# Gated linear attention, a mixer and two MLPs on one core: the first batch in whole 128-token chunks, weight conversion in single steps

## Chip, core and metric

The kernel runs on one core of one Trainium2 chip. The metric is device time in microseconds, the median of several runs; the matrix engine is TensorE (PE in the profile, its weight loads PEld), the others are VectorE (DVE), ScalarE (ACT), GpSimd (POOL) and SyncE (SP), whose queue issues the DMAs.

## What is computed

Attention over 4 batches of 8 heads, 768 tokens, 48 values a head, with a state that decays by a sigmoid gate; then a low-rank mixing over the tokens (rank 32) and an MLP 384 to 1536 to 384, both with a residual; then a gated MLP with width 1024. Cut to what matters:

```python
f = 1.0 / (1.0 + np.exp(-f_logit))
for t in range(S):
    state = f[:, :, t, :, None] * state + einsum('bhd,bhe->bhde', k[:, :, t], v[:, :, t])
    y[:, :, t] = einsum('bhd,bhde->bhe', q[:, :, t], state)
u = x + (x^T @ U @ V)^T                      # x: y of all heads side by side
x = u + max(u @ w_ch1, 0) @ w_ch2            # first MLP
h = max(x @ w_in, 0)                         # second MLP
out = (h * sigmoid(conv3(h) * conv_w)) @ w_out
```

The weights arrive as 64-bit floats, the rest as 32-bit floats.

## The kernel before

**Attention** works in 24 chunks of 128 tokens, six to a batch. For a chunk g, `gates` makes ln(1 + exp(-f)) on ScalarE, `prefix` sums it over the tokens with a triangular matmul into `n`. VectorE evicts `b` (a clamp), ScalarE takes exp from the same bank (`a`), then exp of `b`; GpSimd multiplies q by `a` (`qh`) and k by `b` (`kh`). `transpose` turns both (`qTp`, `kTp`) and ScalarE copies them out. The sums restart at the middle of a chunk: each chunk is two halves of 64 tokens with a state update each, and `scores`, `state` and `values` work in 64 x 64 quarters of the array, two heads and two halves apart. A head's v is needed on both partition halves, so a second copy `vs` with the halves exchanged is loaded. The last row of `a` of each half goes to DRAM (`ends`) and comes back over the partitions (`ends_back`, `ga`) as the state's decay. `mix_in` multiplies the chunk's y by U into `z` and transposes it into `u32`; after six chunks `mix_z` and six `mix_out` add the mixing. All of it is a generator, `chunk(i)`, that yields after each step: seven to a chunk.

**Weights.** A 128-column piece of a 64-bit weight (393 KB) is made into a 32-bit float by three integer instructions on VectorE (L117 to L119), split into two parts by a copy on ScalarE and a subtraction on GpSimd. `Queue.tick(n)` writes n of these steps and the split of the piece before; two pieces are loaded ahead into three buffers. Conversion and attention share the instruction streams in the order in which this is written; nothing reorders it.

**Lead.** In the first stretch attention alone is written, chunks 0 to 5 and the mixing of batch 0, one conversion step after each yield: 54 steps. `fill` adds a matmul that computes nothing needed ahead of transposes and mixing, from the eleventh step on.

**First MLP.** Units of `up1` (tile `a`, then `rh` on ScalarE, `rl` on VectorE) and `down1` (tiles `b`), in 12 pieces j of 128 columns, two tokens' tiles a batch: 512 and 256 tokens for batch 0, 384 twice after that. Nine matmuls a half unit. A half unit ends in a yield, where the main loop writes conversion steps (three as long as there are any), checks of the weights' range, and attention steps of the next batch by a running budget `due`. Before batch 3's units the rest of attention is written and the weights of the second MLP begin to be converted.

**PSUM** has eight banks; `rot` deals out those that transposes, prefix sums and mixing share, two of them (7 and 3) in the lead.

Of the kernel before, what the change touches and what calls it, by code (L numbers as in the profile page):

```python
# [20 lines left out]
LEAD = 1  # L21
# [11 lines left out]
def kernel(  # L33
# [23 lines left out]
    NG = B * NCH  # L57
    N_WHOLE = LEAD * NCH + 2
    NP = H // 2
# [407 lines left out]

    rots = [[7, 3]]

# [41 lines left out]
    ft, qt, kt, vt, vs = {}, {}, {}, {}, {}  # L511
    sph, spl, bt = {}, {}, {}

    def load(dst, src, nm, g):
        if g >= NG:
            return
        b, c = divmod(g, NCH)
        t = {"v": ld_v, "f": ld_f}.get(nm, ld_p).tile([128, H, D], F32, tag=nm, name=nm)
        nc.sync.dma_start(out=t, in_=src[b, :, c * C:(c + 1) * C, :].rearrange("h t d -> t h d"))
        dst[g] = t  # L520
        if nm == "v":


            t = ld_v.tile([128, NP, D], F32, tag="vs", name="vs")
            sv = src[b].rearrange("(a j) t d -> j t a d", j=2)
            for j in range(2):
                at = c * C + (1 - j) * HC
                nc.sync.dma_start(out=t[j * HC:(j + 1) * HC], in_=sv[j, at:at + HC])
            vs[g] = t
# [8 lines left out]
    def gates(g):  # L538
        if g >= NG:
            return  # L540
        sp = spt.pop(g)
        nc.scalar.activation(out=sp, in_=sp, func=ACTF.Exp, scale=-1.0)
        nc.scalar.activation(out=sp, in_=sp, func=ACTF.Ln, bias=one, scale=1.0)

        if g < N_WHOLE:
            sph[g] = sp
            return
        h_ = wk1.tile([128, H, D], F32R, tag="sph", name="sph")
        l_ = wk1.tile([128, H, D], F32R, tag="spl", name="spl")
        nc.scalar.copy(out=h_, in_=sp)  # L550
        sph[g], spl[g] = h_, l_
        sub(nc.vector if g < 4 else nc.gpsimd, l_, sp, h_.bitcast(F32))

    def fill(ps, n=1):


        m, cols = ps.shape[0], min(math.prod(ps.shape[1:]), NCH * 2 * R)
        flat = ps.rearrange("p a b -> p (a b)") if len(ps.shape) == 3 else ps
        for _ in range(n if filling[0] else 0):
            mm(flat[:, 0:cols], tri_r[:, 0:m], uhl.rearrange("p c r -> p (c r)")[:, 0:cols], True, True)  # L560

    filling = [False]

    def prefix(g):
        n = bank(rot(), [128, DM], "n")
        if g >= N_WHOLE:
            mm(n, tri_r, sph.pop(g).rearrange("p h d -> p (h d)"), True, False)
            mm(n, tri_r, spl.pop(g).rearrange("p h d -> p (h d)"), False, True)
        else:
            mm(n, tri, sph.pop(g).rearrange("p h d -> p (h d)"), True, True)  # L570
        nv = n.rearrange("p (h d) -> p h d", h=H)
        b_ = wk1.tile([128, H, D], F32, tag="b", name="b")
        nc.vector.tensor_scalar(out=b_, in0=nv, scalar1=EXP_LIMIT, scalar2=None, op0=ALU.min)
        nc.scalar.activation(out=heads(a_t[g % 2]), in_=nv, func=ACTF.Exp, scale=-1.0)  # L574
        eng = nc.vector if g < 2 else nc.gpsimd
        eng.tensor_tensor(out=heads(q_t[g % 2]), in0=qt.pop(g), in1=heads(a_t[g % 2]), op=ALU.mult)  # L576

        def rest():
            nc.scalar.activation(out=b_, in_=b_, func=ACTF.Exp)
            eng.tensor_tensor(out=heads(k_t[g % 3]), in0=kt.pop(g), in1=b_, op=ALU.mult)  # L580

        return rest
# [9 lines left out]
    def ends(g):  # L592
        for x in range(2):
            r = (x + 1) * HC - 1
            nc.sync.dma_start(out=ends_d[g, x], in_=a_t[g % 2][r:r + 1].rearrange("o p d -> o (p d)"))

    def ends_back(g):
        with nc.allow_non_contiguous_dma(reason="rows over the partitions"):
            nc.sync.dma_start(out=ga[0:MP, g, :], in_=ends_d[g].rearrange("x o (p d) -> d (x o p)", d=128)[0:MP])

    qT, kT, sc, pt, wt, yt = {}, {}, {}, {}, {}, {}

    def transpose(g, nm):
        src, dst = (q_t[g % 2], qT) if nm == "qT" else (k_t[g % 3], kT)
        ps = bank(rot(), [MP, NP, C], nm + "p")
        fill(ps)
        for p in range(NP):
# [13 lines left out]
    def scores(g):  # L621

        kk, qq = kT.pop(g), qT[g]
        ps = bank(2 if g <= LEAD * NCH else 4, [128, NP, 2, HC], "s")
        for p in range(NP):
# [9 lines left out]
    def state(g):  # L635
        kh, vv = k_t[g % 3], vt[g]
        last = (g + 1) % NCH == 0
        ps = [bank((0 if g < LEAD * NCH else 4) + x, [MP, NP, D], f"kv{x}") for x in range(1 if last else 2)]
        for x in range(len(ps)):
# [22 lines left out]
    def values(g):  # L662
# [15 lines left out]
        for j in range(2):  # L678
            nc.scalar.copy(out=av[:, :, j, :], in_=ps[j].rearrange("t (p d) -> t p d", d=D))
        if g < LEAD * NCH:  # L680
            return
        h_ = wk1.tile([128, DM], F32R, tag="xh", name="xh")
# [3 lines left out]
        xh[g], xl[g] = h_, l_  # L686

    zps = {}

    def mix_in(g):  # L690
        b, c = divmod(g, NCH)
        if c == 0:
# [8 lines left out]
        ps = bank(rot(), [128, KD, C], "xT")  # L701
        fill(ps)
        for m in range(KD):
# [27 lines left out]
    def mix_out(b, i):  # L731
        m, hf = divmod(i, 2)
        ps = bank(rot(), [128, HF], "mix")
        fill(ps, 1 if i else 4)
        mm(ps, zst[b][:, m * 128:(m + 1) * 128], vst[:, hf * HF:(hf + 1) * HF], True, True)
# [59 lines left out]
    def chunk(i):  # L795
# [5 lines left out]
        if new:  # L801
            values(i - 1)
            yield
# [37 lines left out]
        if new:  # L841
            for x in range(2 * KD):
                mix_out(i // NCH - 1, x)
                yield
                if x > 1 and x % 2 == 0 and (i == NCH or LEAD == 1):
                    parts["split_tile"](i // NCH - 1, 0, [x // 2 - 1])
            if i == NCH or LEAD == 1:
                parts["split_tile"](i // NCH - 1, 0, [KD - 1])
# [4 lines left out]
    def attention():  # L853
        for i in range(NG + 1):
            yield from chunk(i)

    with tc.manual_schedule():
# [4 lines left out]
            compare_op=ALU.is_ge, fill=0.0,  # L862
        )
        nc.gpsimd.memset(tri[0:HC, HC:C], 0.0)
        nc.vector.memset(one, 1.0)
# [6 lines left out]
        nc.vector.memset(k_t[0], 0.0)  # L872
        nc.vector.tensor_copy(out=tri_r, in_=tri)
        for t, x in ((q_t[1], 0.0), (k_t[1], 0.0), (a_t[1], 1.0), (k_t[2], 0.0)):
            nc.gpsimd.memset(t, x)
# [29 lines left out]
        gates(2)  # L905

        att = attention()
        for n in range(10 ** 6):
            next(att)
            weights.tick(1)  # L910
            filling[0] = n > 10
            if len(mixed) == LEAD:
                break
        filling[0] = False
        rots[0] = [7, 0]
# [6 lines left out]
        late_q = None  # L922
        running = True
        for what, b in half_units:
            if what == "tile":
# [4 lines left out]
                else:  # L930
                    while running and len(mixed) < b + LEAD:
                        if next(att, "end") == "end":
                            running = False
                    left_att, left_hu = n_att if b + LEAD < B else 0, 4 * J1
                assert b in mixed
                if b == B - LEAD:
                    while running and next(att, "end") != "end":
                        pass
                    weights.flush()
                    assert not weights.left()  # L940
                    for _ in checks:
                        pass

                    nc.vector.tensor_reduce(out=g1[:, 0:1], in_=ga.rearrange("p g a -> p (g a)"), axis=mybir.AxisListType.X, op=ALU.min)
                    nc.vector.tensor_reduce(out=g1[:, 1:2], in_=bad, axis=mybir.AxisListType.X, op=ALU.max)
                    nc.vector.scalar_tensor_tensor(
                        out=g1[:, 0:1], in0=g1[:, 1:2], scalar=0.0, in1=g1[:, 0:1], op0=ALU.is_equal, op1=ALU.mult)
                    gs.close()
                    ws_p = ws.enter_context(tc.tile_pool(name="ws_p", bufs=2))
                    weights = Queue(ws_p, parts["open_late"]())  # L950
                    weights.fetch(2)
                continue
            left_hu -= 1
            if LEAD > 1 and left_hu == 10 and b < B - 1:
                parts["split_tile"](b + 1, 0)
            if b >= B - LEAD:
                if left_hu < 4 * J1 - 6 or b > B - LEAD:
                    weights.tick(2 if LEAD == 1 else 1)
                if b == B - LEAD and left_hu == 4 * J1 - 8:
                    ps = bank(rot(), [1, 128], "gp")  # L960
# [11 lines left out]
            if not busy:  # L972
                next(checks, None)
            due += (0.6 if busy else left_att / max(left_hu - 4, 1))
            while due >= 1 and left_att > 0 and running:
# [181 lines left out]
```

## Time and profile before

| | us |
|---|---|
| median of three runs | 719.91 |
| lowest, highest | 719.77, 720.64 |
| the profiled execution | 719.37 |
| its span in the profile | 717.4 |
| first matmul of the first MLP | 93.48 |
| first matmuls of the second MLP | 502 |

| engine | busy us | share |
|---|---|---|
| TensorE | 681.3 | 95% |
| VectorE | 450.4 | 63% |
| ScalarE | 298.1 | 42% |
| GpSimd | 148.4 | 21% |

Matmuls overlap, so a busy TensorE is not yet one at its peak. The chain that ended last is TensorE for 81% of the span, VectorE for 9%, ScalarE for 4%.

### The profile page before, as it was taken

What the parts mean: (1) busy time and instruction counts of PE and PEld (TensorE: products, weight loads), DVE (VectorE), ACT (ScalarE), POOL (GpSimd) and SP (SyncE); (2) the same over time, 40 slices, a digit from 0 to 9 for tenths busy, and PEclk for the clock granted to TensorE, in tenths of its full rate; (3) what the DMA queues carried; (4) which work ended last, traced back from release to release, by engine and by line L of the source; (5) the groups of instructions that cost most, each with busy time, mean ns of one, the idle gap of its engine ahead of it and who ended that gap; (6) DMA issues with size and microseconds to landing.
All of it is one profiled execution on the core that took longest, in us unless ns stands there. A gap on an engine that the chain in (4) does not pass through costs nothing.

```text
span 717.4 us, 15034 instructions
## 1 busy us (share of the span) xinstructions
PE 681.3 (95%) x6260; PEld 627.0 (87%) x6260; DVE 450.4 (63%) x749; ACT 298.1 (42%) x608; POOL 148.4 (21%) x147
## 2 busy tenths in 40 slices
PE   6988789999999999999999999999899999999996
PEld 4656577878899989999998999999899999999996
DVE  5679889334654534444433437888787877877763
ACT  4556443335444434424523213224444544535542
POOL 1246553214222222112300002223001001001000
PEclk9769789999999999999999999999999999999999
DMA  7799754435455254234210102331000100100102
GB/s 153 159 210 209 184 144 99 95 74 113 95 117 128 65 108 93 62 78 102 50 35 2 45 0 67 97 102 45 0 1 1 67 1 0 67 1 1 67 0 71
DMA packets 158000, 53.96 MB, mean 75 GB/s; under 512 B 138012, under 2 KB 153396, under 8 KB 157924
## 3 DMA queue, kind: packets, MB, share of 16 engines
q1 hardware_dynamic: 157924, 52.92, 31.4%
q8 instruction: 51, 0.84, 0.5%
q14 instruction: 25, 0.20, 0.1%
HBM read 48.08 MB, written 4.82 MB: 74 GB/s over the span
## 4 chain that ended last, share of the span: by engine, by line
PE 81%; DVE 9%; ACT 4%; issue 3%; DMA 2%; SPq 1%; POOL 0%; DVEq 0%; ACTq 0%; POOLq 0%
PE a L71 35%; PE b L71 32%; PE y L71 3%; PE s L71 3%; PE kv L71 2%; DVE u L118 1%; DVE ul L74 1%; PE n L71 1%; DMA u<-in_moe_w_ch_dram 1%; PE z L71 1%; PE kTp L608 1%; PE qTp L608 1%; PE xT L704 1%; DVE u L117 1%; DVE u L737 1%
## 5 line engine op out<-in xcount | busy, mean ns | idle before, releaser
L255 DVE SCALAR_TENSOR_TENSOR rl<-a,rh 128x384 fp32r<-128x384 f32 (+2 forms) x96 | 53.4, 556 | 147.9 <-ACT rh L254 147.8
L254 ACT ACTIVATE rh<-a 128x384 fp32r<-128x384 f32 (+2 forms) x96 | 47.1, 490 | 167.7 <-PE a L71 167.5
L71 PE MATMUL a<-uh,w1h 128*128 128x384 f32 (+2 forms) x288 | 103.0, 358 | 3.1 <-DVE rl L255 1.4
L71 PE MATMUL b<-rh,w2h 128*128 128x384 f32 (+2 forms) x288 | 101.1, 351 | 0.0
L71 PE MATMUL a<-ul,w1h 128*128 128x384 f32 (+2 forms) x288 | 97.9, 340 | 0.0
L71 PE MATMUL a<-uh,w1l 128*128 128x384 f32 (+2 forms) x288 | 97.7, 339 | 0.0
L71 PE MATMUL b<-rh,w2l 128*128 128x384 f32 (+2 forms) x288 | 97.0, 337 | 0.0
L71 PE MATMUL b<-rl,w2h 128*128 128x384 f32 (+2 forms) x288 | 96.6, 336 | 0.0
L71 PE MATMUL b<-woh,w1h 128*128 128x384 f32 x264 | 70.4, 334 | 0.0
L71 PE MATMUL a<-uh,winh 128*128 128x384 f32 x192 | 65.7, 342 | 1.8 <-ACT h L307 1.8
L71 PE MATMUL a<-ul,winh 128*128 128x384 f32 x192 | 66.1, 344 | 1.1 <-DVE ul L74 1.1
L71 PE MATMUL a<-uh,winl 128*128 128x384 f32 x192 | 65.8, 343 | 0.0
L71 PEld LDWEIGHTS a<-uh,w1h 128*128 128x128 f32 x288 | 54.4, 189 | 8.0 <-DVE u L737 2.6
L74 POOL TENSOR_TENSOR ul<-u,uh 128x384 fp32r<-128x384 f32 (+2 forms) x16 | 19.6, 1232 | 201.7 <-ACT uh L95 201.7
L71 PEld LDWEIGHTS b<-rh,w2h 128*128 128x128 f32 x288 | 54.2, 188 | 2.6 <-issue 0.3
L71 PEld LDWEIGHTS a<-uh,w1l 128*128 128x128 f32 x288 | 54.4, 189 | 1.7
L71 PEld LDWEIGHTS a<-ul,w1h 128*128 128x128 f32 x288 | 54.5, 189 | 1.2
L71 PEld LDWEIGHTS b<-rh,w2l 128*128 128x128 f32 x288 | 54.1, 188 | 1.5
L71 PEld LDWEIGHTS b<-rl,w2h 128*128 128x128 f32 x288 | 54.3, 189 | 1.1
L313 ACT ACTIVATE c<-c 128x768 f32<-128x768 f32 x31 | 26.3, 847 | 64.8 <-DVE c L343 64.8
L576 POOL TENSOR_TENSOR qh<-q,a 128x384 f32<-128x384 f32 x22 | 23.9, 1086 | 137.5 <-ACT a L574 117.2
L71 PEld LDWEIGHTS b<-woh,w1h 128*128 128x128 f32 x264 | 48.0, 188 | 0.0
(154 smaller groups left out, 1409.1 us busy)
## 6 DMA issues: line engine op xcount, KB each, us to landing
u<-in_moe_w_ch_dram SPq DMA_DIRECT2D x24, 384.0 KB
raw<-in_moe_w_ch_dram SPq DMA_DIRECT2D x24, 384.0 KB
f<-in_f_logit_dram SPq DMA_DIRECT2D x24, 192.0 KB
k<-in_k_dram SPq DMA_DIRECT2D x24, 192.0 KB
q<-in_q_dram SPq DMA_DIRECT2D x24, 192.0 KB
v<-in_v_dram SPq DMA_DIRECT2D x24, 192.0 KB
out_dram<-o SPq DMA_DIRECT2D x24, 192.0 KB
raw<-in_moe_w_in_dram SPq DMA_DIRECT2D x8, 384.0 KB
```

The source lines that it names most:

```text
L71: nc.tensor.matmul(out=out, lhsT=lhsT, rhs=rhs, start=start, stop=stop, skip_group_check=True)
L74: eng.tensor_tensor(out=out, in0=a, in1=b, op=ALU.subtract)
L117: lambda: ve.tensor_scalar(out=t, in0=hi, scalar1=3, scalar2=0x3FFFFFFF, op0=ALU.logical_shift_left, op1=ALU.bitwise_and),
L118: lambda: ve.scalar_tensor_tensor(out=t, in0=hi, scalar=-(1 << 30), in1=t, op0=ALU.bitwise_and, op1=ALU.bitwise_or),
L254: nc.scalar.activation(out=rh, in_=ps, func=ACTF.Relu)
L255: nc.vector.scalar_tensor_tensor(out=rl, in0=ps, scalar=0.0, in1=rh.bitcast(F32), op0=ALU.max, op1=ALU.subtract,)
L313: nc.scalar.activation(out=c, in_=c, func=ACTF.Sigmoid)
L576: eng.tensor_tensor(out=heads(q_t[g % 2]), in0=qt.pop(g), in1=heads(a_t[g % 2]), op=ALU.mult)
L608: nc.tensor.transpose(out=ps[:, p, :], in_=src[:, p, 0:MP], identity=ident)
L704: nc.tensor.transpose(out=ps[:, m, :], in_=x[:, m * 128:(m + 1) * 128], identity=ident)
L737: nc.vector.tensor_tensor(out=dst, in0=ps, in1=dst, op=ALU.add)
```

## The change

Batch 0 (`N_WIDE`, six chunks) is taken out of the generator and written by a new function `wide(i)`. There a chunk is whole: the prefix sums run over all 128 tokens, `scores_wide` makes 128 x 128 scores for two heads at a time on halves of the array, each head row with its bank and mask (`mask_wide`), `state_wide` updates the state once, `values_state` and `values_chunk` make y in two parts. `vs` and the first `ends` are not loaded and stored for these chunks. `prefix` is written ahead of the two masks, and a chunk holds three conversion steps instead of about seven. The first MLP starts after the same point of chunk 7 as before. In the main loop attention steps count 0.25 for each half unit instead of 0.6 as long as weights are left, range checks go twice as fast, and the second MLP's weights begin from within batch 3's units. The fillers are gone. Gates 6 and 7 are split in two like the later ones. The core of the diff (the new functions whole but for `state_wide`'s and `values_out`'s ends):

```diff
-    N_WHOLE = LEAD * NCH + 2
+    N_WIDE = LEAD * NCH
-    rots = [[7, 3]]
+    rots = [[0, 1]]
-        if nm == "v":
+        if nm == "v" and g >= N_WIDE:
-    def fill(ps, n=1):
...
     def ends(g):
         for x in range(2):
+            if x == 0 and g < N_WIDE:
+                continue
...
-        ps = bank(2 if g <= LEAD * NCH else 4, [128, NP, 2, HC], "s")
+        ps = bank(4, [128, NP, 2, HC], "s")
...
+    def scores_wide(g):
+        kk, qq = kT.pop(g), qT[g]
+        ps = sw[g] = [bank(2 + j, [128, NP, C], f"s{j}") for j in range(2)]
+        for p in range(NP):
+            for j in range(2):
+                mm(ps[j][:, p, :], kk[rows(j), p, :], qq[rows(j), p, :], True, True)
+        pt[g] = []
+
+    def mask_wide(g, j):
+        t = wk2.tile([128, NP, C], F32, tag="p", name="p")
+        nc.vector.tensor_tensor(
+            out=t, in0=sw[g][j], in1=tri.unsqueeze(1).to_broadcast([128, NP, C]), op=ALU.mult)
+        pt[g].append(t)
+
+    def state_wide(g):
...
+        ps = src = bank(7, [MP, NP, D], "kv")
+        for p in range(NP):
+            for j in range(2):
+                m = 64 if j == 0 else D
+                mm(ps[64 * j:64 * j + m, p, :], kh[:, p, 64 * j:64 * j + m], vv[:, 2 * p + j, :], True, True)
...
+    def values_state(g):
+        ps = yw[g] = [bank(4 + j, [128, NP * D], f"y{j}") for j in range(2)]
+        qq = qT.pop(g)
+        if g % NCH:
+            w = wt.pop(g)
+            for p in range(NP):
+                for j in range(2):
+                    mm(ps[j][:, p * D:(p + 1) * D], qq[rows(j), p, :], w[rows(j), p, :], p == 0, False)
+
+    def values_chunk(g):
+        ps, vv, pp = yw[g], vt.pop(g), pt.pop(g)
+        for j in range(2):
+            for p in range(NP):
+                mm(ps[j][:, p * D:(p + 1) * D], pp[j][:, p, :], vv[:, 2 * p + j, :],
+                   p == 0 and g % NCH == 0, p == NP - 1)
...
+    def wide(i):
+        load(kt, k, "k", i + 3)
+        load(qt, q, "q", i + 3)
+        load(ft, f_logit, "f", i + 4)
+        load(vt, v, "v", i + 2)
+        if i > 0:
+            values_out(i - 1)
+        scores_wide(i)
+        if i + 2 < NG:
+            second = prefix(i + 2)
+        mask_wide(i, 0)
+        mask_wide(i, 1)
+        state_wide(i)
+        gate_max(i + 3)
+        if i + 2 < NG:
+            ends(i + 2)
+        weights.tick(1)
+        if i + 1 < NG:
+            transpose(i + 1, "qT")
+            transpose(i + 1, "kT")
+        if i + 2 < NG:
+            second()
+        gates(i + 3)
+        values_state(i)
+        weights.tick(1)
+        if i > 0:
+            mix_in(i - 1)
...
+        values_chunk(i)
+        weights.tick(1)
+        if i + 2 < NG:
+            ends_back(i + 2)
...
-        for i in range(NG + 1):
+        for i in range(N_WIDE, NG + 1):
             yield from chunk(i)
...
+        for i in range(N_WIDE):
+            wide(i)
+        rots[0] = [7, 0, 1]
         att = attention()
-        for n in range(10 ** 6):
+        while len(mixed) < 1:
             next(att)
             weights.tick(1)
-            filling[0] = n > 10
...
-                    left_att, left_hu = n_att if b + LEAD < B else 0, 4 * J1
+                    left_att, left_hu = n_att + (10 if b + LEAD == B - 1 else 0) if b + LEAD < B else 0, 4 * J1
...
-                if left_hu < 4 * J1 - 6 or b > B - LEAD:
-                    weights.tick(2 if LEAD == 1 else 1)
+                since += 1
+                if since > 2:
+                    weights.tick(2)
...
             if not busy:
                 next(checks, None)
+                next(checks, None)
-            due += (0.6 if busy else left_att / max(left_hu - 4, 1))
+            due += (0.25 if busy else left_att / max(left_hu - 4, 1))
```

How the instructions stand. First VectorE in the lead, in one chunk: `p` is the masked scores, `b` the eviction of the prefix sums, `sp` the gates' clamp, `u32` the buffer in which L117 to L119 convert. Before:

```order
L630 TENSOR_TENSOR p_645<-s_628,msk_98 128x512
L118 SCALAR_TENSOR_TENSOR u32_63<-u32_63 128x384
L573 TENSOR_SCALAR b_650<-n_648 128x384
L536 TENSOR_SCALAR sp_656<-f_479 128x384
L119 SCALAR_TENSOR_TENSOR u32_63<-u32_63 128x384
L117 TENSOR_SCALAR u32_63<-u32_63 128x384
```

After (two lines further up in the file, so that L116 to L118 convert):

```order
L562 TENSOR_SCALAR b_637<-n_634 128x384
L691 TENSOR_TENSOR p_641<-s0_624,tri_96 128x512
L691 TENSOR_TENSOR p_643<-s1_625,tri_96 128x512
L706 TENSOR_TENSOR wtmp_654<-kv_645,w_550 112x192
L708 TENSOR_TENSOR w_656<-wtmp_654,ga_99 112x192
L535 TENSOR_SCALAR sp_658<-f_512 128x384
L116 TENSOR_SCALAR u32_63<-u32_63 128x384
L117 SCALAR_TENSOR_TENSOR u32_63<-u32_63 128x384
L118 SCALAR_TENSOR_TENSOR u32_63<-u32_63 128x384
```

The eviction `b` has moved ahead of the masks, conversion steps have moved from between them to the chunk's end.

Second, SP's queue in the lead, from one `ends_back` on. Before, to the next one:

```order
L599 DMA ga_99<-ends_d_106 112x8x1
L519 DMA k_475<-in_k_dram 128x8x48
L519 DMA q_477<-in_q_dram 128x8x48
L519 DMA f_479<-in_f_logit_dram 128x8x48
L106 DMA u32_63<-in_moe_w_ch2_dram 128x768
L595 DMA ends_d_106<-a0_111 1x512 x2
L519 DMA v_555<-in_v_dram 128x8x48
L528 DMA vs_557<-in_v_dram 64x4x48 x2
L106 DMA u32_63<-in_moe_w_ch1_dram 128x3x256
L599 DMA ga_99<-ends_d_106 112x8x1
```

After, up to the one weight load of the chunk:

```order
L591 DMA ga_99<-ends_d_106 112x4x1
L518 DMA k_410<-in_k_dram 128x8x48
L518 DMA q_412<-in_q_dram 128x8x48
L518 DMA f_414<-in_f_logit_dram 128x8x48
L518 DMA v_416<-in_v_dram 128x8x48
L586 DMA ends_d_106<-a0_111 1x512
L105 DMA u32_63<-in_moe_w_ch2_dram 128x768
```

`vs` and one of the two `ends` are gone, `v` has moved to the other loads, and one weight load is left of two or three.

Third, VectorE in the first MLP tile, between the `rl` of the eighth and of the ninth up unit. Before (`raw` and `bad` are a range check, `wtmp` and `w` the state):

```order
L255 SCALAR_TENSOR_TENSOR rl_1704<-a_1705,rh_1703 128x512
L165 TENSOR_TENSOR raw_1665<-raw_1665 128x384
L652 TENSOR_TENSOR wtmp_1736<-kv0_1718,w1_1464 112x192
L654 TENSOR_TENSOR w0_1738<-wtmp_1736,ga_99 112x192
L652 TENSOR_TENSOR wtmp_1740<-kv1_1719,w0_1738 112x192
L654 TENSOR_TENSOR w1_1742<-wtmp_1740,ga_99 112x192
L167 SCALAR_TENSOR_TENSOR bad_105<-raw_1665,bad_105 128x384
L630 TENSOR_TENSOR p_1785<-s_1768,msk_98 128x512
L255 SCALAR_TENSOR_TENSOR rl_1788<-a_1789,rh_1787 128x512
```

After:

```order
L254 SCALAR_TENSOR_TENSOR rl_1327<-a_1328,rh_1326 128x512
L118 SCALAR_TENSOR_TENSOR u32_63<-u32_63 128x384
L116 TENSOR_SCALAR u32_63<-u32_63 128x384
L117 SCALAR_TENSOR_TENSOR u32_63<-u32_63 128x384
L118 SCALAR_TENSOR_TENSOR u32_63<-u32_63 128x384
L116 TENSOR_SCALAR u32_63<-u32_63 128x384
L117 SCALAR_TENSOR_TENSOR u32_63<-u32_63 128x384
L254 SCALAR_TENSOR_TENSOR rl_1370<-a_1371,rh_1369 128x512
```

At this place, where conversion was over before, there are now two pieces' three steps, and the attention steps have moved to later units.

## Rows read from the trace of the kernel before

**Rows 1.** The page's 40 slices of 17.9 us: granted clock and DMA in tenths, GB/s.

```profile
PEclk9769789999999999999999999999999999999999
...
DMA  7799754435455254234210102331000100100102
...
GB/s 153 159 210 209 184 144 99 95 74 113 95 117 128 65 108 93 62 78 102 50 35 2 45 0 67 97 102 45 0 1 1 67 1 0 67 1 1 67 0 71
```

**Rows 2.** Single microseconds: busy us and instructions of each engine, clock, DMA share, GB/s.

```profile
16.00:17.00 1.00, 0.02 (x1) 0.02 (x1) 1.00 (x3) 0.90 (x2) 0.00 (x0) 1.00 1.24 218
...
17.00:18.00 1.00, 1.00 (x3) 0.50 (x4) 0.29 (x2) 0.00 (x0) 0.00 (x0) 0.77 0.71 129
...
27.00:28.00 1.00, 1.00 (x10) 0.92 (x7) 0.56 (x1) 0.99 (x3) 0.62 (x1) 0.61 1.04 203
...
37.00:38.00 1.00, 0.00 (x0) 0.00 (x0) 0.70 (x2) 0.00 (x0) 0.65 (x1) 1.00 0.78 130
...
51.00:52.00 1.00, 1.00 (x7) 0.84 (x5) 0.97 (x2) 0.94 (x3) 0.96 (x1) 0.66 0.93 179
```

**Rows 3.** TensorE in order of time, the scores: start us, us, instruction.

```profile
14.21 1.15 PE L71 MATMUL s<-qT,kT 48*64 48x64 f32 x32
...
44.52 1.97 PE L71 MATMUL s<-qT,kT 48*64 48x64 f32 x32
...
54.47 1.15 PE L71 MATMUL s<-qT,kT 48*64 48x64 f32 x32
...
71.79 1.14 PE L71 MATMUL s<-qT,kT 48*64 48x64 f32 x31
```

**Rows 4.** The chain of waits in the lead: start us, us, what.

```profile
33.22 4.05 DMA u<-in_moe_w_ch_dram
...
44.59 1.90 PE s L71 x32
...
46.50 1.58 PE n L71 x2
...
50.55 0.85 PE qTp L608 x4
...
93.48 3.49 PE a L71 x9
```

**Rows 5.** The chain of waits in the first MLP tile.

```profile
113.78 2.36 PE a L71 x9
...
116.15 1.08 PE s L71 x32
...
117.22 2.28 PE b L71 x9
...
124.05 1.08 PE y L71 x64
...
132.49 0.87 PE kv L71 x27
```

**Rows 6.** Groups by line and form on VectorE, 0 to 93.5 us.

```profile
L119 DVE SCALAR_TENSOR_TENSOR u<-u 128x384 int32<-128x384 int32 x15 | 11.9, 795 | 0.2
...
L118 DVE SCALAR_TENSOR_TENSOR u<-u 128x384 int32<-128x384 int32 x16 | 10.9, 684 | 0.3
...
L117 DVE TENSOR_SCALAR u<-u 128x384 int32<-128x384 int32 x16 | 8.6, 535 | 1.5 <-DMA u<-in_moe_w_ch_dram 1.4
...
L630 DVE TENSOR_TENSOR p<-s,msk 128x512 f32<-128x512 f32 x8 | 5.5, 682 | 1.3 <-PE s L71 1.3
```

**Rows 7.** VectorE in order of time, first MLP tile: three of its rl.

```profile
101.40 0.69 DVE L255 SCALAR_TENSOR_TENSOR rl<-a,rh 128x512 fp32r<-128x512 f32 x1 [0.22 <-ACT rh L254]
...
106.31 0.68 DVE L255 SCALAR_TENSOR_TENSOR rl<-a,rh 128x512 fp32r<-128x512 f32 x1
...
117.24 0.68 DVE L255 SCALAR_TENSOR_TENSOR rl<-a,rh 128x512 fp32r<-128x512 f32 x1
```

**Rows 8.** Busy time of each engine from 122 to 165 us, columns as in rows 2.

```profile
122.00:165.00 43.00, 42.02 (x487) 33.79 (x486) 17.30 (x34) 18.25 (x41) 12.10 (x12) 1.00 0.37 77
```

## What the change will do to the time

> **What bounds the kernel now.** I read the 40 slices first, then the single microseconds around each change of clock, then the chain of waits, then single instructions. The slices [rows 1] show two kernels in one. From the fifth or sixth slice to the end (18 us each) TensorE is near its peak at the full clock, and the second MLP, from 501 us on, is not touched by the change. In the first five slices the clock is mixed, the DMA engines are 70 to 90% and more busy and move up to 210 GB/s. In this **lead** (0 to 93.5 us, when the first matmul of the first MLP starts [rows 4]) nothing of the MLP runs: batch 0 goes through attention alone, and every microsecond taken out of it is taken out of the total unless it comes back later.
>
> The six chunks of batch 0 start their scores at 14.2, ..., 44.5, 54.5, and chunk 6 at 71.8 [rows 3]: 57.6 us for six, 9.6 each. TensorE is not what needs so long at the full clock: one chunk's matmuls there take s 1.08, y 1.08, kv 0.87 [rows 5], and half of the cold prices of n 1.58, z (as many columns, in float32 too: the same) and two transposes of 0.85 [rows 4], with three quarters of 0.43 for xT: 5.8 us, and the fillers. Two things stretch it. The weights' conversion is woven between the mask and the eviction `b` of the prefix sums, so that a late weight (4.05 us of waiting at 33.2 [rows 4]) stops `b`, then the exp behind it, then the transposes: TensorE does nothing from 37 to 38 us [rows 2], and its clock falls to 1.2 GHz. And at that clock it is itself the bound. Read from the mean clock of single microseconds [rows 2]: idle from 16 to 17, half clock from 17.5 (0.77) to 27.8 (0.61); idle from 37, half clock to 51.7 (0.66).
>
> **The change, part by part.** *Chunks of batch 0 whole.* Scores: 16 matmuls of 64 columns on quarters of the array become 8 of 128 columns on halves. The quarter form runs two at a time (even and odd head use other rows and other columns); if the halves do so too, columns times count is the same: 1.08 us. If not, 2.16. Of halves the trace has nothing; I take 1.08, the nearest row. On this the Trainium skill (TensorEngine Tiling (Array Packing), Key Properties) says that different tiles can execute weight loads and matmuls in parallel; by it 1.08 holds, without it the sum would be 6 x 1.08 = 6.5 us worse, at half clock more. The quarters' rows agree with it; no row here has halves. kv: half the matmuls, 0.44. y: 8 on halves for the state, 8 on the whole array for the chunk; between 1.08 (all of y now) and two records for each of 8 at the transposes' 0.11, 1.7, plus 0.5 for the state, 2.2: I take 1.5. n 0.79, transposes 0.85, z 0.79, xT 0.32. Sum at full clock 5.8 us, at half clock 10 (s 1.90 against 1.08 [rows 4, 5]).
>
> *VectorE.* A piece of weights is three steps, 0.54 + 0.68 + 0.80 = 2.0 us [rows 6]. The lead made 54 steps (18 pieces: U, two of V, 15 weights); now it makes 3 in each of six chunks and 14 in chunk 6: 32 steps, 7 weights. Per chunk that is one piece in place of 2.3, 2.7 us less; one mask more, 0.68; one add and one product of the state less. So VectorE has at least 2 us less per chunk than today, where it kept up: no bound. Each step also loses its place ahead of `b`: the order printed above has `b` first. What is late next is TensorE itself.
>
> *DMA.* A chunk loaded f, k, q, v and vs, 197 KB each, and 2.3 pieces of 393 KB: 1.9 MB, 9 us at 210 GB/s [rows 1]; that alone nearly explains 9.6 us. It now loads four of the five and one piece: 1.18 MB, 5.6 us. On SP's queue go two vs issues, one ends issue and 1.3 weight loads per chunk; the weights are fetched two pieces, now two chunks, ahead, so the wait at 33.2 goes.
>
> *Fillers* (24 matmuls): nothing waits for them but TensorE itself. What they may have held up is the clock: second rival.
>
> **The lead's length.** Chunk 0: the idle microsecond before 17 is not changed (it ends with the ln of the third gates), so n starts at 17 and the clock falls as before. Then at half clock n 1.6, kv 0.8, transposes 1.7, the chunk's y 1.9: chunk 1 starts at 23.0 (now 21.7; y moved into the own chunk). Half clock lasted 10.3 us the first time [rows 2]; I take 10.5, so chunk 1 costs s and n cold (3.5), then mostly warm: 9.3 us, to 32.3. Four more at 5.8 plus 1.3 for waits that stay (kT's bank waits for `b` and the exp; changes between array shapes): 7.1 each, 60.7. Today 71.8: 11.1 us earlier. Ends: 5.4 + 0.9 from 31 us on gives 56.2 (15.6 earlier); 8.5 from 34 on gives 68 (3.8 earlier). From there to the first MLP matmul, 93.5 - 71.8 = 21.7 us, the same 14 conversion steps, six mixing adds and splits stand on VectorE: no gain taken; ends 1 us either way.
>
> **What the first MLP tile gives back.** 17 pieces are left where 9 were: 17 half units (a or b of one 128-column slice) instead of about 10 carry three steps each. From one rl to the next, a pair of half units, VectorE needs 4.9 us, and 10.9 for the next two pairs, with one state update of four instructions among them [rows 7]: 5.3 on average. TensorE needs 2.36 + 2.28 = 4.6 [rows 5] plus half an attention step (0.25 per half unit instead of 0.6), 0.3: 4.9. So today's 4.5 to 5 such pairs cost 0.4 to 1.9 us over TensorE's need, 8.5 pairs cost 3.4; the half clock at the tile's start (first group of nine at 3.49 instead of 2.36 [rows 4, 5]) stays as it is. I take a difference of 2.5. Lower end 0: with less attention in it a pair may come down to 4.5 on VectorE. Upper end 8: each pair at 5.8, as if every step met GpSimd's subtraction (of the 16 us that eight pieces of 2.0 take, half would then have nothing of TensorE beside it).
>
> Attention moved out of that tile comes later at 1.55 steps per half unit instead of 1.18. The work on TensorE is the same and it is busy for 42.0 of the 43 us from 122 to 165 [rows 8], so I add 1 us for tighter waits (0 to 3). The range checks at double rate meet a VectorE that is busy for 17.3 of those 43: nothing, and without that cover up to 1 us. The late weights that start three half units earlier, and the longer budget before the last batch, only spread work: nothing.
>
> **Sum.** The profiled execution took 719.37 us (span 717.4). 719.4 - 11.1 + 2.5 + 1.0 = 711.8. The median of the three runs is 0.5 above that execution: 712.3.
>
> **The rivals.** *One: the tile gives it all back.* VectorE is the bound for 17 half units near the upper price, and chunks of 8 us shorten the lead by only 7: -7 + 6 + 1, 719.9, that is 717 to 722. For it: today's pairs already run at VectorE's pace [rows 7]. Against: the two pairs and the state update of 10.9 us contain 9.3 of TensorE's own, so under 1 us a pair is at stake. *Two, slower: the lead stays at half clock.* Without fillers the clock that falls at 17.5 does not come back before the MLP. Then chunk 1 starts at 23 and five chunks take 10 us plus 1.3 each: 79.5, 7.7 later than now; 719.9 + 7.7 + 3.5 = 731. It decides from an average chunk of 9.8 us. For it: the clock needed ten microseconds, nearly all of them busy, to come back. Against: it did come back, at 27.8 before any filler had run, after work of the same kinds. The Trainium skill (TensorE: Matmul & The Clock Gate, What's actually happening) has the throttled state as the default and activity as what releases it; by it the missing fillers speak for this rival and the denser chunks against, and the time would be 731 or 712 accordingly. *Three: more than that.* Halves run beside each other and y is at its lower price, transfers no longer wait, the six chunks take 6.3 each: 15.6 off, 2.5 back, 706 to 707; with a tile that costs nothing, 704.
>
> **How the numbers follow.** Forecast 60%: 707 to 718. Rival one 18%: 717 to 722. Rival two 10%: 726 to 734. Rival three 12%: 703 to 707. 0.2% is 1.4 us, about what a measurement here can tell. Faster: 0.60 + 0.12 and a third of rival one, 0.77. Same: half of rival one, 0.10. Slower: rival two and the rest, 0.13. For 8 in 10 the range leaves out rival two and the best of rival three: 704 to 721.
>
> **What would show it.** Right: chunk 6's scores near 61 us, half clock ending before 30 us and not returning before the mixing, no VectorE wait for a weight in the lead, first MLP matmul near 82, and in the tile 17 half units at 2.5 us with rl queued behind six steps. Wrong: chunk starts more than 8 us apart after 32 us (then see whether the clock, the DMA share or VectorE is full); s over 1.3 us at full clock (halves not side by side); a half unit over 2.8 us, or TensorE idle in 170 to 210 us where attention now is denser.

## Result, and the profile after

| | us |
|---|---|
| before, median of four runs beside it | 720.09 |
| after, median of four runs (lowest, highest) | 729.74 (726.69, 732.12) |
| ratio after / before, 95% interval | 1.0131 (1.0092 to 1.0169) |
| the profiled execution of after, its span | 729.66, 727.9 |
| first matmul of the first MLP | 86.17 (before 93.48) |

The changed kernel is 1.3% slower; the forecast was 712.3 (704 to 721). Ratios here and below leave out a run that is over 1.5% above the fastest of its kernel, which is one run in all, of 721.20 us, of the kernel called no load. The page's slices (TensorE's granted clock in tenths, share of the DMA engines, GB/s) and its chain, to be held against [rows 1]:

```profile
PEclk9799599999979999999999999999999999999999
DMA  7788455466435565302100102331000000100102
GB/s 141 155 169 186 120 159 143 92 143 139 115 99 134 119 143 106 61 1 41 23 14 2 43 1 66 93 104 44 0 1 1 34 32 1 66 1 1 65 1 70
PE 71%; DVE 10%; issue 8%; ACT 4%; DMA 4%; POOL 2%; SPq 0%; ACTq 0%; DVEq 0%; POOLq 0%
PE a L70 30%; PE b L70 27%; PE y L70 4%; DMA raw<-in_moe_w_ch_dram 3%; PE s L70 3%; DVE ul L73 1%; PE kv L70 1%; DVE u L117 1%; PE n L70 1%; PE kTp L601 1%; DVE u L118 1%; PE z L70 1%; DVE rl L254 1%; DVE bad L166 1%; DVE raw L164 1%
```

Two things are new. The twelfth slice (200 to 218 us) has a clock of 0.7, deep in the first MLP, where before it was full. And in the chain stand `raw` (the load of a range check, 3%) and the check's two instructions, L164 (the product) and L166 (the comparison); none of the three is in this row of the page of before.

**Where it was lost.** The first MLP makes 96 `rl`, 24 to a batch, the same in both kernels, so they serve as mileposts. The first comes at 97.6 us before and 90.8 after, the 13th at 165.6 and 150.1: after leads by 15.5 us in the middle of batch 0's tiles. The 25th, batch 1's first, comes at 210.9 and 221.6: after is 10.7 behind, and it stays so to the end (10.5 in the span). The whole loss, 26 us of milepost, lies between the 13th and the 25th. The two stretches as windows (from:to, length, busy us and instructions of PE, PEld, DVE, ACT, POOL, then clock, DMA share, GB/s):

```profile
90.80:150.10 59.30, 57.11 (x463) 45.69 (x465) 48.05 (x84) 24.40 (x52) 26.20 (x25) 1.00 0.53 135
150.10:221.60 71.50, 60.37 (x818) 53.40 (x810) 35.91 (x75) 27.95 (x67) 18.32 (x19) 0.90 0.53 119
```

In the second TensorE is idle for 11.1 us and its clock is 0.90. Attention that the change moved there explains a part of its length, but not 11 us of idle time. What VectorE waits for from 90 to 430 us says more (waiting instruction, what ended the wait, us in all, times, longest):

```profile
DVE rl L254 <- ACT rh L253: 113.1, 56, 4.8
DVE raw L164 <- DMA raw<-in_moe_w_ch_dram: 21.6, 14, 2.9
```

The first row is VectorE with nothing to do and costs nothing. The second is new: before, in the same stretch, no wait of VectorE was for this load. One such wait, VectorE in order of time (start, us, instruction, the idle time before it):

```profile
192.98 0.42 DVE L254 SCALAR_TENSOR_TENSOR rl<-a,rh 128x256 fp32r<-128x256 f32 x1 [3.52 <-ACT rh L253]
195.15 0.56 DVE L164 TENSOR_TENSOR raw<-raw 128x384 f32<-128x384 f32 x1 [1.75 <-DMA raw<-in_moe_w_ch_dram]
195.75 0.56 DVE L166 SCALAR_TENSOR_TENSOR bad<-raw,bad 128x384 f32<-128x384 f32 x1
196.22 0.54 DVE L810 TENSOR_TENSOR zt<-z,zt 32x384 f32<-32x384 f32 x1
197.34 0.55 DVE L73 TENSOR_TENSOR zst<-zt,zst 32x384 fp32r<-32x384 f32 x1 [0.58 <-ACT zst L814]
197.91 0.36 DVE L646 TENSOR_TENSOR w<-kv,ga 112x192 f32<-112x192 f32 x1
```

The check's product stands for 1.75 us on its load, and the eviction of the mixing sums (`zt`, `zst`) stands behind it on VectorE, though its input has long been there. TensorE needs `zst` for the mixing. The same microseconds on TensorE:

```profile
190.00:195.00 5.00, 3.95 (x55) 3.28 (x54) 0.42 (x1) 3.88 (x9) 2.76 (x3) 1.00 0.55 138
195.00:200.00 5.00, 1.60 (x9) 1.07 (x8) 4.07 (x9) 1.20 (x3) 0.00 (x0) 0.90 0.39 79
200.00:205.00 5.00, 5.00 (x21) 4.39 (x20) 2.63 (x7) 0.79 (x2) 0.00 (x0) 0.50 0.04 9
205.00:210.00 5.00, 4.75 (x46) 4.27 (x46) 2.58 (x5) 1.19 (x3) 1.31 (x1) 0.57 0.84 191
```

3.4 us of idle time from 195 to 200 us, and behind them ten microseconds at 1.2 GHz: the starved TensorE loses twice. TensorE's longest waits in the second stretch:

```profile
PE s L70 <- DVE wtmp L644: 2.9, 2, 2.4
PE mix L70 <- DVE zst L73: 2.4, 1, 2.4
PE qTp L601 <- ACT a L563: 1.8, 1, 1.8
```

Each of the three longest comes right behind a wait of VectorE for a check's load: 2.15 us up to 169.20, 1.75 up to 195.15 and 2.88 up to 218.04. What VectorE does next is `wtmp`, `zt` with `zst`, and `b`, behind which ScalarE makes `a` from the same bank. Together they are 6.6 of the 11.1 us.

### The profile page after: what moved, and what is told of

Read it like the earlier page. It is cut to its first block, busy times and chain, and to the rows that moved or that the text cites. A ratio compares the mean times of both kernels' runs of the same rounds, so it can differ in the third digit from the quotient of the medians.

```text
span 727.9 us, 14218 instructions
## 1 busy us (share of the span) xinstructions
PE 681.7 (94%) x5852; PEld 631.3 (87%) x5852; DVE 451.5 (62%) x743; ACT 298.6 (41%) x610; POOL 149.0 (20%) x150
## 4 chain that ended last, share of the span: by engine, by line
PE 71%; DVE 10%; issue 8%; ACT 4%; DMA 4%; POOL 2%; SPq 0%; ACTq 0%; DVEq 0%; POOLq 0%
PE a L70 30%; PE b L70 27%; PE y L70 4%; DMA raw<-in_moe_w_ch_dram 3%; PE s L70 3%; DVE ul L73 1%; PE kv L70 1%; DVE u L117 1%; PE n L70 1%; PE kTp L601 1%; DVE u L118 1%; PE z L70 1%; DVE rl L254 1%; DVE bad L166 1%; DVE raw L164 1%
## 5 line engine op out<-in xcount | busy, mean ns | idle before, releaser
L70 PE MATMUL a<-ul,w1h 128*128 128x384 f32 (+2 forms) x288 | 99.4, 345 | 0.0
L565 POOL TENSOR_TENSOR qh<-q,a 128x384 f32<-128x384 f32 x22 | 22.2, 1009 | 144.2 <-ACT a L563 129.7
```

The costliest lines, as they stand in the source:

```text
L70: nc.tensor.matmul(out=out, lhsT=lhsT, rhs=rhs, start=start, stop=stop, skip_group_check=True)
```

## The experiments

All times are medians, ratios are to the kernel before, run beside them; "checks" are the range checks. Theory A: VectorE waits, in order, for the check's load. Theory B: the attention pushed out of the tile's first half crowds the second. C and D are told where they come up.

**Checks once**, the one line undone:

```diff
-                next(checks, None)
                 next(checks, None)
```

> The changed kernel, with one step of the range checks for each half unit as before the change, so that a check's load has two half units until its product instead of one. Theory A (VectorE stands in order behind the check's load; what queues behind it starves TensorE and costs it the clock): the 21.6 us that VectorE waits for the checks' loads fall under 2, TensorE's idle between the 12th and 24th rl falls from 11 to about 3 us, the half clock from 200 to 210 us is gone; 729.7 - 10 to 15, that is 714 to 720. Theory B (the attention that was pushed out of the first half of the tile crowds the second half, 1.55 steps for each half unit): the checks hardly matter, 726 to 730.

710.77 us (709.21 to 711.70), ratio 0.9881 (0.9863 to 0.9899): 19 us below the changed kernel (17 below its second measurement, further down), and faster than the kernel before. VectorE's wait for the loads, and the stretch between the 13th and 25th `rl` (145.8 to 202.8 us):

```profile
DVE raw L164 <- DMA raw<-in_moe_w_ch_dram: 2.5, 5, 0.8
```

```profile
145.80:202.80 57.00, 53.59 (x815) 48.09 (x807) 28.85 (x63) 28.06 (x67) 19.06 (x19) 1.00 0.51 108
```

57.0 us instead of 71.5: 7.7 of the 14.5 less are idle time, the other 6.8 TensorE's busy time, nearly the same instructions at full clock (1.00 against 0.90). Of the three waits of TensorE above none is left. The gain is above A's range (10 to 15 us); that A counted too little of the clock is the likely reason, but no run separates it.

**Both undone**, checks once and 0.6 attention steps, and **early attention alone**, with checks at the double rate:

```diff
-            due += (0.25 if busy else left_att / max(left_hu - 4, 1))
+            due += (0.6 if busy else left_att / max(left_hu - 4, 1))
```

> The changed kernel with checks once and 0.6 attention steps: both undone. The two theories agree on the sum and differ in whether it adds to either alone: A expects what checks once gives, within 2 us (714 to 720); B what early attention gives, within 2 us. If each costs a part, it is below both by that part. The lead's 7 us are then all that is left of the change, less the conversion in the first tile: 712 to 716 if nothing else comes back.

> The changed kernel, with 0.6 attention steps for each half unit as long as weights are left, as before the change, instead of 0.25; checks at the double rate stay. Theory B: the second half of the tile is then as dense as before the change (about 1.2 steps) and the loss between the 12th and 24th rl goes: 716 to 720, less what the first half of the tile gives back by holding more (1 to 3 us). Theory A: the waits for the checks' loads stay (about 20 us of VectorE), 726 to 731.

713.63 (ratio 0.9916, 0.9894 to 0.9938) and 732.19 (1.0173, 1.0101 to 1.0244). B falls: alone, early attention helps nothing, and beside checks once it costs some 3 us. Later attention, which the prediction charged with 1 us, is a gain of this size.

**Load ahead**: double rate, but the next load is issued right behind the comparison, two half units before its product.

```diff
-        for load, *rest in items:
-            raw, p, n = load(pool, *rest)
+        ahead = [items[0][0](pool, *items[0][1:])]
+        for i in range(len(items)):
+            for _ in range(4):
+                yield
+            raw, p, n = ahead.pop()
...
-            yield
-            yield
...
-            yield
...
-            yield
+            if i + 1 < len(items):
+                ahead.append(items[i + 1][0](pool, *items[i + 1][1:]))
```

> The changed kernel, with checks at the double rate and the same instructions, but the next check's load is issued right behind the last instruction of the one before, two half units ahead of its product. Only the wait is taken away. Theory A: like the kernel with checks once, 714 to 720, VectorE's wait for the checks' loads under 2 us. Theory B, or a theory in which the checks' two VectorE instructions or their transfers at twice the rate are what costs: 725 to 730.

719.70 (717.39 to 724.17), 1.0014 (0.9990 to 1.0037). It didn't do what it was for:

```profile
DVE raw L165 <- DMA raw<-in_moe_w_ch_dram: 23.3, 18, 3.1
```

The wait is as long as ever, though the time fell by 8 to 10 us, which I can't explain; this run doesn't tell A from the others. Why the wait stayed, the trace shows. There is one buffer, so a load is not issued before the comparison is through; a comparison that waited makes the next load late, and that makes VectorE wait again:

```profile
176.91 0.56 DVE L166 SCALAR_TENSOR_TENSOR bad<-raw,bad 128x384 f32<-128x384 f32 x1
177.49 0.37 SPq L105 DMA_DIRECT2D raw<-in_moe_w_ch_dram  x1
181.01 0.88 DVE L165 TENSOR_TENSOR raw<-raw 128x384 f32<-128x384 f32 x1 [1.88 <-DMA raw<-in_moe_w_ch_dram]
```

A second buffer was not tried.

**No read**: both instructions at the double rate and all loads, but the instructions work on `bad` itself.

```diff
-            nc.vector.tensor_tensor(out=hi, in0=hi, in1=hi, op=ALU.mult)
+            own = bad[0:p, 0:n]
+            nc.vector.tensor_tensor(out=own, in0=own, in1=own, op=ALU.mult)
...
-            nc.vector.scalar_tensor_tensor(out=bad[0:p, 0:n], in0=hi, scalar=LEAST_HIGH * LEAST_HIGH, in1=bad[0:p, 0:n], op0=ALU.is_lt, op1=ALU.max)
+            nc.vector.scalar_tensor_tensor(out=own, in0=own, scalar=-1.0, in1=own, op0=ALU.is_lt, op1=ALU.max)
```

> The changed kernel with checks at the double rate, all their loads and both VectorE instructions, but these work on the tile that gathers the result and not on what was loaded: the range of the weights is not checked. The transfers and VectorE's work stay, the wait for the transfer is gone altogether. Theory A (the wait in VectorE's order): 708 to 713, as with checks once or a little less, since its 2.5 us of such waits go as well. Theory D (the transfers at twice the rate slow attention's own loads, or two more VectorE instructions for each half unit are too many): 718 to 730.

715.34 (710.68 to 721.26), 0.9954 (0.9915 to 0.9993). This takes away VectorE's wait (and the next load's wait for the buffer), and 0.0176 of the ratio goes, 12.7 us: A holds for about two thirds of the loss. Some 5 us over checks once stay, and the result lies between A's and D's ranges. The ten runs spread over 10.6 us with the mean granted clock: 0.983 in the fastest, 0.970 in the slowest, and 0.013 of 720 us is 9.4 us. In its profile the stretch reads

```profile
146.70:208.10 61.40, 55.53 (x811) 49.29 (x803) 35.61 (x74) 27.91 (x67) 18.80 (x19) 0.97 0.59 138
```

with 6.8 us more of VectorE than with checks once, 2.5 more of idle TensorE and a clock of 0.97.

**No load**: the same two instructions at the double rate, without loads. **No checks**: neither. (As in no read, the range is not checked.)

```diff
         for load, *rest in items:        # no checks: items[:0]
-            raw, p, n = load(pool, *rest)
...
+            own = bad[:, 0:384]
...
```

> The changed kernel with the two VectorE instructions of each check at the double rate, on the tile that gathers the result, and with no loads for them at all: the range of the weights is not checked. Beside the kernel that loads but doesn't read (715.3 us, from 710.7 to 721.3, with half clock for 4 us in its profile): if its remainder over checks once (4.5 us) is the transfers, this one is 708 to 712; if it is the two extra instructions for each half unit on VectorE, it stays at 714 to 717.

> The changed kernel with no range checks at all, neither loads nor instructions: the floor under the checks. Checks once cost 2.5 us of VectorE's waits and 1.2 us of its work for every four half units: 707 to 710 if even that costs a little, 710 to 712 if checks once are free, as the prediction had it.

No load 714.51 (710.54 to 721.20), no checks 709.42 (ratio 0.9865, 0.9835 to 0.9895). Checks once cost about 1 us over none (0.9881 against 0.9865, within the intervals). The median without loads is the one with them (714.5 and 715.3), which speaks for VectorE's instructions as the remainder; but its four runs spread as wide, and its ratio of 0.9905 (0.9869 to 0.9941) overlaps both. Its kept profile, of the run of 721.20 us, has the same stretch at

```profile
150.10:213.10 63.00, 57.12 (x814) 50.76 (x807) 35.67 (x75) 27.97 (x67) 18.91 (x19) 0.95 0.33 59
```

6 us longer than with checks once, 5.9 of it idle as in no read (3.4 with checks once), and no check's load is in it. There the remainder needs no transfers. That is one profile, so what makes the last 2 to 5 us stays open, VectorE's instructions being the likelier.

**Before, checks twice**, the one line added to the kernel before:

```diff
                 next(checks, None)
+                next(checks, None)
```

> The kernel before with one edit: checks at the double rate. If the doubling costs by itself: the same waits of some 20 us on VectorE, and 8 to 19 us more than before, 728 to 739. Theory C (the doubling costs only where attention's steps are as dense as the change makes them, 1.55 for each half unit against 1.18 here): within 4 us of before, 719 to 724, although VectorE waits for the loads here too.

737.08 (735.79 to 741.99), 1.0262 (1.0211 to 1.0313): 18.3 us more than before (718.82). The doubling costs by itself what it costs in the changed kernel, so theory C, which made the denser attention a condition, falls. The wait is there too:

```profile
DVE raw L165 <- DMA raw<-in_moe_w_ch_dram: 27.4, 13, 3.9
```

**Second tile**: no checks until batch 1, then at the double rate.

```diff
-            if not busy:
+            if not busy and b > 0:
```

> The changed kernel with no checks in the tiles of batch 0; they begin with batch 1, at the double rate. The trace of the changed kernel loses nothing from batch 1's first rl to batch 2's (111.6 us against 112.0 before) though VectorE waits some 10 us for loads there. Theory A with C (a wait costs only where TensorE has no slack left in what attention hands it): 707 to 711, at most that of checks once. If every wait of VectorE for a load costs, wherever it stands: 720 to 729.

716.10 (713.56 to 720.43), 0.9959 (0.9938 to 0.9979), above what A with C gave and below what a price on every wait gave. Its waits only moved:

```profile
DVE raw L164 <- DMA raw<-in_moe_w_ch_dram: 37.6, 19, 3.2
```

```profile
146.90:202.80 55.90, 53.24 (x813) 47.82 (x805) 22.54 (x50) 28.01 (x67) 18.78 (x19) 1.00 0.40 75
202.80:322.40 119.60, 113.87 (x1272) 105.24 (x1271) 66.84 (x130) 44.44 (x98) 25.17 (x25) 0.99 0.51 121
```

Batch 0's second half is at its best, and batch 1 takes 119.6 us where checks once take 110.3 (202.8 to 313.1). So waits cost in batch 1 too. What one costs isn't a fixed share of it, though: here 37.6 us of waits cost 9.3 us of batch 1, while in the changed kernel batch 1 held 13.1 us of waits and lost 1.3 (111.6 against 110.3), and batch 0's second half held 8.5 and lost 14.5 (71.5 against 57.0), the clock with it. In after again, which comes next, that half held 12.1 and lost 15.2. By the three waits of TensorE above it depends on whether something that TensorE needs soon stands behind the wait; a rule for it these runs don't give.

**After again**, unedited:

> The changed kernel once more, unedited, for its lead: the four kernels so far share its lead to the letter and start the first MLP at 82.6 to 82.8 us with the clock at full speed from 17 to 29 us, while the profile of the changed kernel has half clock there and starts it at 86.2. If that is chance from run to run, runs spread over 4 us and the profile may show either; if it belongs to the kernel, it is again 86.

727.98 (727.51 to 729.67), 1.0129 (1.0100 to 1.0159): the same time, with another lead, as the next section shows.

**Two edits on top of checks once.** Short tail: no conversion between the mixing adds of the lead. Fill tail: matmuls that compute nothing while TensorE waits there.

```diff
+            steps += 1
-            weights.tick(1)
+            if steps < 8:
+                weights.tick(1)
```

```diff
+        for _ in range(0 if b else 4 if i else 12):
+            mm(ps, tri_r, uhl.rearrange("p c r -> p (c r)")[:, 0:HF], True, True)
```

> The changed kernel with checks once, and without the conversion steps between the six mixing adds of the lead (seven steps, two to three pieces more for the first tile). In the trace of checks once VectorE works through 68 to 82 us with these steps between the adds while TensorE waits for them twice (1.8 and 2.5 us). The first MLP matmul comes 3 to 5 us earlier than 82.8, and the tile gives back 0.5 to 2 us: 706 to 710. If the conversion is the bound in the tile, all comes back: 710 to 712.

> The changed kernel with checks once, and matmuls that compute nothing (12 of 384 columns before the first mixing product of the lead, 4 before each other) in the 3.3, 1.8 and 2.5 us where TensorE waits there. If they hold the clock, the half clock from 67 to 85 us goes: y, n and the first nine of the first tile are 2 to 3 us shorter, 707 to 709. If VectorE is what that stretch waits for, nothing moves or the fillers stand in the way: 710 to 713.

711.73 (708.03 to 714.77) and 711.26 (709.45 to 713.27), neither told from checks once. Short tail does begin the MLP 3.9 us earlier:

```profile
78.91 0.79 PE L70 MATMUL a<-uh,w1h 128*128 128x512 f32 x1
```

but by the 25th `rl` it has given that back (202.4 us in its profile, 202.8 with checks once): the tile pays for every piece that it gets. Fill tail does hold the clock from 72 to 82 us:

```profile
72.00:77.00 5.00, 4.00 (x21) 3.49 (x21) 4.86 (x11) 0.96 (x3) 1.01 (x1) 1.00 0.46 115
77.00:82.00 5.00, 2.26 (x39) 1.83 (x37) 4.63 (x8) 1.59 (x4) 2.28 (x2) 1.00 0.29 82
```

(0.50 in both with checks once), but VectorE is busy for 9.5 of these 10 us, and from chunk 6's scores to the first `a` it takes 22.5 us (63.80 to 86.28) as with checks once (60.34 to 82.78: 22.4). VectorE is the bound there, and a faster TensorE only waits more. No kernel here that computes everything is shown to be faster than the changed one with checks once.

## Why the prediction was wrong, step by step

**The step that failed** is "The range checks at double rate meet a VectorE that is busy for 17.3 of those 43: nothing, and without that cover up to 1 us" [rows 8]. It measured 17 to 19 us (729.7 and 728.0 against 710.8), of which 12.7 go with the wait; some 5 stay without it, with the instructions and the transfers at the double rate, so they were not free either. The prediction priced the checks as work alone, and asked only whether VectorE has room. But the generator yields twice between load and product: at one step a half unit the load has two half units to land, at two steps one. A half unit of batch 1 is 2.3 us (111.6 for 48). A load needs more; its issue on SP's queue and the product that waits for it, in the changed kernel and with checks once:

```profile
165.31 0.56 SPq L105 DMA_DIRECT2D raw<-in_moe_w_ch_dram  x1
...
169.20 0.56 DVE L164 TENSOR_TENSOR raw<-raw 128x384 f32<-128x384 f32 x1 [2.15 <-DMA raw<-in_moe_w_ch_dram]
```

```profile
152.00 0.40 SPq L105 DMA_DIRECT2D raw<-in_moe_w_ch_dram  x1
...
156.88 0.81 DVE L164 TENSOR_TENSOR raw<-raw 128x384 f32<-128x384 f32 x1
```

3.9 us from issue to product against 4.9 with no wait. Other products of the changed kernel that waited start 3.0 us (195.15, load issued at 192.13) to 4.1 us (237.54, issued at 233.41) behind the issue. The issue itself can be late: the one at 192.13 stands on SP's queue behind `ends`, `v` and `vs`, and `ends` began at 189.74, when the `a` that it stores was done. The trace of before could have shown it: a load of the same 393 KB stands in the chain for 4.05 us from its issue at 33.22 us [rows 4]. The prediction took these 4.05 us for a wait of VectorE, but VectorE stood for 0.66 of them:

```profile
37.30 0.57 DVE L117 TENSOR_SCALAR u<-u 128x384 int32<-128x384 int32 x1 [0.66 <-DMA u<-in_moe_w_ch_dram]
```

The Trainium skill (DMA: Bandwidth & Descriptors, Anatomy of one DMA) has a fixed 2.0 us and a part by size; by it this load is an estimated 2.9 us, over a half unit too, though the page measured DMAs that GpSimd issues; the rows here are longer, by up to 1.2 us. And the working never asked what is queued behind the product on VectorE: `rl`, the `b` of the prefix sums, `zst`. Idle time of TensorE in this stretch was at least named as what would show it wrong.

**The rest of the sum held, in part by luck.** Forecast 712.3 with the checks at nothing; with checks at their old rate it is 710.8.

*The lead, -11.1.* The profile of after has -7.3. It spent 18 to 29 us at half clock (mean 0.53), as forecast: chunk 1 starts at 23.23 us and chunk 2 at 33.06, and chunk 6, at 63.72 and not 60.7, is late mostly by the price of a chunk. But that was that execution; the same instructions in after again were not at half clock (1.00):

```profile
18.00:29.00 11.00, 11.00 (x70) 9.35 (x67) 4.85 (x12) 4.87 (x12) 2.85 (x3) 0.53 0.61 127
```

```profile
18.00:29.00 11.00, 10.75 (x117) 8.63 (x117) 7.85 (x16) 7.59 (x18) 4.93 (x5) 1.00 0.60 128
```

In after again chunk 6's scores start at 60.03 us (forecast 60.7) and the first `a` at 82.47 (forecast 82), -11.0. That is luck: two errors cancel. Half clock from 17.5 for 10.5 us, taken over from before, did not come in that run, so chunk 1 started at 21.5, not 23.0, and chunk 2 at 29.4, not 32.3. And a chunk takes 7.5 to 7.9 us, not 7.1, and TensorE is busy for all but 0.2 of it. One chunk of after again:

```profile
29.38 1.16 PE L70 MATMUL s<-qT,kT 48*128 48x128 f32 x16
30.47 0.91 PE L70 MATMUL n<-sp,tri 128*128 128x384 f32 x2
31.31 0.67 PE L70 MATMUL kv<-v,kh 128*64 128x48 f32 x16
31.91 0.65 PE L601 MATMUL qTp<-ident,qh 128*112 128x128 f32 x4
32.72 0.62 PE L601 MATMUL kTp<-ident,kh 128*112 128x128 f32 x4 [0.16 <-ACT a L563]
33.27 1.10 PE L70 MATMUL y<-w,qT 48*128 48x48 f32 x16
34.29 0.83 PE L70 MATMUL z<-x,u_f 128*32 128x384 f32 x2
35.06 0.55 PE L793 MATMUL xT<-ident,x 128*128 128x128 f32 x3
35.44 1.88 PE L70 MATMUL y<-v,p 128*128 128x48 f32 x16
37.25 1.16 PE L70 MATMUL s<-qT,kT 48*128 48x128 f32 x16
```

s is 1.16 (taken 1.08; 2.16 if not side by side): the halves do run side by side. The Trainium skill (TensorEngine Tiling (Array Packing), Key Properties) says that different tiles can execute weight loads and matmuls in parallel, and this row agrees. y is mis-sized: 1.10 and 1.88, 2.98 against 1.5 and over its upper end of 2.2. Its chunk part is a little over the upper price of 1.7; its state part was priced at 0.5 by its few columns, but its 16 records of 48 columns on halves take 0.07 us each, as the 16 of s with 128 columns do: there it is the record that costs, not the column. kv is 0.67 against 0.44: 0.04 us for each of its 16 records, where the sum took half of the 0.87 us that the same state took on quarters [rows 5], in records of 0.03. The two transposes are 0.65 and 0.62 against 0.43 each. The waits of 1.3 are 0.2.

*The tile, +2.5, and later attention, +1.* With checks once the stretch from the first to the 25th `rl` is 116.2 us against 113.3 before, +2.9 for both together; forecast +3.5. The signs inside differ: with attention at its old pace it is 119.7, so eight pieces more cost some 6 us (2.5 in the sum, 0 to 8 its range), and later attention gives 3 back (a cost of 1 in the sum, 0 to 3 its range). That the two add up to the forecast is luck again.

*Late weights and longer budget, nothing:* from batch 2's first `rl` to the span's end 394.4 us with checks once (from 313.1), 394.5 before (from 322.9).

*The rivals.* Rival two, the slower one, gave 731 and the result is 729.7, but not by its mechanism: the chunks are warm without fillers. The chance of a slower kernel hung on the wrong place. Rival three's 706 to 707 leaves out the 1.0 for later attention: by its own terms it is 707.8.

## What to carry to other kernels

Doubling the rate of a loop that loads, yields and uses also halves the time its load has to land: hold issue to use against the time between two steps, not the instructions against the engine's idle share. On an engine that works in order, a wait for a transfer is paid by all that is written behind it, and again in clock if it starves TensorE. When a kernel changes many things, undo the edit that was priced at nothing first: here one line was worth 17 to 19 us and hid a gain of 1.2%.

## What the runs showed that I had not expected

The half clock at 18 to 29 us is a matter of chance: of twelve profiles that share this part of the lead, the first one of after and those of no load and fill tail have it (0.53) and the other nine don't (1.00), for the same instructions. TensorE stands idle for 1.6 us ahead of it in all twelve, up to 16.6 to 17.4 us. But in the three chunk 0's scores begin at 13.85 to 13.93 us and in the nine at 14.15 to 14.65, so that an earlier start by some tenths goes with the fall. It moves the first `rl` from 86.4 to 87.4 us to 90.8 to 91.0, 4 us (short tail, whose lead is shorter, aside). The Trainium skill (TensorE: Matmul & The Clock Gate, What's actually happening) says that activity is watched in windows that run on freely and don't restart with the kernel, so that the point of a change varies; that agrees with the spread, though no run here shows the cause.

In no read and no load, runs of one kernel spread over 10 us, and the mean clock goes with them (no read: 710.7 us at a mean of 0.983, 721.3 at 0.970); the four runs of checks once spread over 2.5. The half clock in the lead can be 4 us of it. In no read's profile, which doesn't have that, the clock falls in the first MLP instead (0.97 from 146.7 to 208.1 us). What decides it there is not shown.
